# Attention ahead of two matrix stages: keys loaded a chunk earlier, x and operand casts placed later, one chunk's output stage in units of three blocks

## The chip, the cores and the metric

The kernel runs on one core of a Trainium2 chip. The metric is the device time of one execution in microseconds (us). The core has five engines with an instruction queue each: PE (matrix multiply), DVE (vector), ACT (scalar, activation tables), POOL (GpSimd) and SP, which here issues every DMA transfer. An engine works its queue off in order; an instruction that waits holds everything behind it on the same engine. Engines wait for each other, and for DMA landings, by semaphores.

## The reference

All arrays are float32; there are 8 batches, 8 heads, 576 positions and 64 values per head.

```python
k_p = k.reshape(B, H, S // 8, 8, D).mean(axis=3)
v_p = v.reshape(B, H, S // 8, 8, D).mean(axis=3)
scores = (1 / np.sqrt(D)) * np.matmul(q, k_p.transpose(0, 1, 3, 2))
attn = np.exp(scores - np.max(scores, axis=-1, keepdims=True))
attn = attn / (np.sum(attn, axis=-1, keepdims=True) + 1e-09)
x = np.matmul(attn, v_p)      # heads joined: x is 4608 x 512
gate = 1.0 / (1.0 + np.exp(-(x @ w_gate)))       # 512 x 1536
x = gate * (x @ w_val) @ w_out                   # 1536 x 512
h = x @ w_in                                     # 512 x 2048
out = (h * np.cos(h)) @ w_out2                   # 2048 x 512
```

## The kernel before

The 4608 tokens are worked in nine chunks of 512, called c = 0 to 8; a chunk boundary does not fall on a batch boundary, so a chunk's attention uses the keys of two batches. A float32 product is made of three PE passes: each operand is split into a high part (a cast, "high") and the rest (a subtraction, "low", always by the helper on line 65), and high x high, high x low and low x high are added in PSUM. Except where the inputs are still plain, the large products use a scheme with 7 block products in place of 8, so sums and differences of operand blocks are formed on DVE and POOL, written to DRAM and fetched back.

The stages follow each other on PE.

- **Attention with gate and value** (to 521 us). For chunk c the function `half_steps(c)` walks 12 half-steps; each is 12 matmuls of 128x512 (one block of the gate, `pg`, or of the value product, `pv`). After each half-step's matmuls stand the pieces that `plan(c+1)` puts there for the attention of the next chunk: loads of q, k and v (`q_load`, `kv_load`), pooling of eight rows (`kv_pool`, on POOL), transposing the pooled keys (`k_step`: PE `pk` and `pkr`, then DVE `kbd`), scores (`psc`), softmax, the transposed weights (`a_step`: `pa`, `par` to `aT`), the product with the values (`x_step`: `px`, split to `xT`, in two pieces) and the casts of the pooled values (`v_step`: `vm`, `vRp`, `vr`). A piece has a half-step number and, inside it, a priority; `put_early` places one in the window before. SP, POOL, ACT and DVE get their instructions in that same written order. The block results g are stored to `od`; of every second one POOL forms four differences `tg` (four instructions on line 755, in a tile with one buffer), whose store is put two half-steps on. The third key load (`raw_k_2`) and the third value load (`raw_v_2`) share the tile tag `kvrest`, which has one buffer.
- **Gate groups** (521 to 806 us): `g_block`, seven products per block of four chunk pairs; its operands xg are fetched, cast on ACT (`x_high`, line 1002) and split on DVE (`x_low`) at places that a table gives as (block, position).
- **w_out units** (806 to 1089 us): `half_step` takes blocks of g (`up`) fetched back from `od` and casts and splits them two blocks at a time. Groups come in the order 1, 0, 2, 3, 4, where group 0 is one chunk alone (256 columns in place of 512). Beside them run steps on the next weights (`i2_begin` and what follows it). Results `ok` are stored to `xd`; `HOMES` names the memory each lies in.
- **h stage** (1089 to 1452 us): `h_block`, the product with w_in of the second layer, then the sine on ACT; operands x by the same two functions at a table's places; sums `s_S` on POOL.
- **y stage** (1452 to 1818 us): `y_chunk`; its weights `wy` are loaded from `yd` by `load_last`, cast by `last_high` on ACT and split by `last_low` on POOL.

## Time and profile before

| | us |
|---|---|
| median of three runs | 1818.41 (1817.71 to 1825.63) |
| the profiled execution | 1819.77 |
| its span from first to last instruction | 1818.0 |

The engines were busy: PE 94 % of the span, DVE 65 %, ACT 52 %, POOL 37 %. PE's granted clock has two levels, 1.2 and 2.4 GHz; the profile gives it as a share of the full one, so 0.50 is 1.2 GHz throughout, and 0.93 over a stretch is a mean. A stretch's idle time of PE is its length less PE's busy time. In a row of the timeline the bracket at the end gives how long the engine stood idle ahead of the row, and what ended that.

### The profile page before, as it was taken

Reading aid. Unit: us, or ns where it says so; the run is one execution under the profiler, and the core shown is the slowest. Engines: PE = TensorE matmul, PEld = TensorE weight load, DVE = VectorE, ACT = ScalarE, POOL = GpSimd, SP = SyncE. Lnnn points to the kernel's source line nnn. Section 1 sums busy time; section 2 is a strip of 40 time slices with the busy share of each in tenths; the row PEclk is TensorE's granted clock in tenths of the full one; section 3 lists DMA queues with packets and bytes.
Section 4 is the critical chain, followed back from the end, with each engine's and each line's share of the span. In section 5 each row is a group of like instructions: output and inputs, shape, how many; then the busy total and the mean of one; then the engine's idle time right before and its main releaser. Section 6 shows DMA issues by size and latency. Waiting matters only on the chain. (4 is left out here: it accounts for less than half of the span.)

```text
span 1818.0 us, 27457 instructions
## 1 busy us (share of the span) xinstructions
PE 1704.9 (94%) x9432; PEld 1427.3 (79%) x9432; DVE 1184.9 (65%) x1775; ACT 951.4 (52%) x1850; POOL 674.5 (37%) x731
## 2 busy tenths in 40 slices
PE   7898998999999898999899998999999989999999
PEld 6776776777788776887778887888887878888887
DVE  7757565655585544566866686677777766565665
ACT  6454444444453443455554476677767854434433
POOL 3556566652363444340000003566757870000000
PEclk8899998999999999999999999999999989999999
DMA  9465567775469676668888876586778887666663
GB/s 255 128 209 167 172 206 246 209 224 169 155 234 307 219 241 227 214 209 285 267 266 275 263 244 211 171 268 207 259 232 290 283 284 251 225 206 218 209 216 124
DMA packets 305195, 411.04 MB, mean 226 GB/s; under 512 B 57504, under 2 KB 235424, under 8 KB 305056
## 3 DMA queue, kind: packets, MB, share of 16 engines
q1 hardware_dynamic: 305056, 409.29, 70.0%
q8 instruction: 75, 1.23, 0.3%
q14 instruction: 64, 0.52, 0.1%
HBM read 235.93 MB, written 173.28 MB: 225 GB/s over the span
## 5 line engine op out<-in xcount | busy, mean ns | idle before, releaser
L1090 POOL TENSOR_TENSOR s_S<-z_a,z_a 128x512 f32<-128x512 f32 (+1 forms) x78 | 99.3, 1294 | 393.5 <-DVE z_a L1074 393.5
L65 DVE TENSOR_TENSOR sp<-sp,sp 128x1024 fp32r<-128x1024 f32 x126 | 152.3, 1249 | 97.2 <-ACT sp L1293 97.2
L65 DVE TENSOR_TENSOR up<-up 128x1024 fp32r<-128x1024 f32 (+1 forms) x105 | 117.7, 1125 | 76.5 <-ACT up L895 75.8
L895 ACT CAST up<-up 128x1024 fp32r<-128x1024 f32 (+1 forms) x105 | 100.7, 964 | 101.2 <-DMA up<-od 80.7
L1380 PE MATMUL py_A<-wy,sp 128*128 128x512 f32 x432 | 135.7, 395 | 0.0
L1039 PE MATMUL pha<-x,hw 128*128 128x512 f32 (+1 forms) x320 | 120.5, 376 | 4.6 <-DVE z_a L1074 2.1
L1293 ACT CAST sp<-sp 128x1024 fp32r<-128x1024 f32 x126 | 123.9, 1056 | 0.0
L1043 PE MATMUL pha<-x,hw 128*128 128x512 f32 (+1 forms) x320 | 118.3, 370 | 0.0
L1044 PE MATMUL pha<-x,hw 128*128 128x512 f32 (+1 forms) x320 | 118.2, 369 | 0.0
L1070 ACT ACTIVATE z_a<-z_a 128x512 f32<-128x512 f32 (+1 forms) x160 | 94.4, 590 | 34.0 <-DVE z_a L1063 32.2
L755 POOL TENSOR_TENSOR tg<-g 128x256 f32<-128x256 f32 x54 | 53.3, 986 | 154.4 <-DMA od<-tg 84.3
L1172 PE MATMUL pga<-xg,gw 128*128 128x512 f32 (+1 forms) x240 | 90.9, 379 | 17.8 <-ACT pg L1206 15.3
L539 ACT ACTIVATE e<-psc,mx 128x72 f32<-128x72 f32 x256 | 57.9, 337 | 90.9 <-DVE mx L535 90.9
L755 POOL TENSOR_TENSOR tg<-g,g 128x256 f32<-128x256 f32 x54 | 52.5, 971 | 139.9 <-DVE g L731 139.6
L1090 POOL TENSOR_TENSOR s_S<-z_a,s_S 128x512 f32<-128x512 f32 (+1 forms) x78 | 96.2, 1233 | 3.4 <-DMA sd<-s_S 0.4
L708 PE MATMUL pg<-xT,wg 128*128 128x512 f32 (+1 forms) x228 | 93.3, 409 | 3.9 <-ACT e L560 2.7
L755 POOL TENSOR_TENSOR tg<-g,tg 128x256 f32<-128x256 f32 x108 | 94.7, 877 | 4.2
L1385 PEld LDWEIGHTS py_A<-wy,sp 128*128 128x128 f32 x432 | 81.1, 188 | 19.2
L708 PE MATMUL pv<-xT,wv 128*128 128x512 f32 (+1 forms) x228 | 94.2, 413 | 0.4 <-DVE g L731 0.4
L918 PE MATMUL po_A<-up,so 128*128 128x512 f32 (+1 forms) x240 | 90.2, 376 | 3.6 <-DVE up L65 3.4
L710 PE MATMUL pg<-xT,wg 128*128 128x512 f32 (+1 forms) x228 | 89.9, 394 | 3.4 <-DVE wg L65 3.4
L917 PE MATMUL po_A<-up,so 128*128 128x512 f32 (+1 forms) x240 | 89.1, 371 | 2.6 <-ACT up L895 2.6
(223 smaller groups left out, 5146.8 us busy)
## 6 DMA issues: line engine op xcount, KB each, us to landing
sp<-sd SPq DMA_DIRECT2D x126, 512.0 KB
up<-od SPq DMA_DIRECT2D x168, 256.0 KB
sd<-s_S SPq DMA_DIRECT2D x128, 256.0 KB
od<-tg SPq DMA_DIRECT2D x54, 512.0 KB
sd<-z_a SPq DMA_DIRECT2D x96, 256.0 KB
raw_o<-in_moe_w_out_dram SPq DMA_DIRECT2D x28, 512.0 KB
xg<-gd SPq DMA_DIRECT2D x28, 512.0 KB
x<-xd SPq DMA_DIRECT2D x28, 512.0 KB
```

Source lines behind the costliest of these rows:

```text
L65: engine.tensor_tensor(out=lo, in0=x, in1=hi.bitcast(F32), op=ALU.subtract)
L708: nc.tensor.matmul(p, wh, x[:, 0, kb], start=kb == 0, stop=False)
L755: nc.gpsimd.tensor_tensor(out=t[:, k], in0=x, in1=y, op=ALU.subtract)
L895: nc.scalar.copy(hi, lo.bitcast(F32))
L1039: nc.tensor.matmul(p, wh, x[:, 0, kb], start=k in (0, 3) and kb == 0, stop=False, skip_group_check=True,)
L1043: nc.tensor.matmul(p, wh, x[:, 1, kb], start=False, stop=False, skip_group_check=True)
L1044: nc.tensor.matmul(p, wl, x[:, 0, kb], start=False, stop=kb == 1, skip_group_check=True)
L1070: nc.scalar.activation(z, z, AF.Sin, scale=TURN)
L1090: engine.tensor_tensor(out=z[name], in0=z[x], in1=z[y], op=op)
L1172: nc.tensor.matmul(p, wh, x[:, 0, kb], start=k in (0, 3) and kb == 0, stop=False, skip_group_check=True,)
L1293: nc.scalar.copy(hi[:, r], lo[:, r].bitcast(F32))
L1380: nc.tensor.matmul(p, x[0][:, m, s], w, start=fresh and m == 0, stop=False, skip_group_check=True,)
```

## The change

- **Attention.** The key loads of chunk c+1 go from the end of the window before and its own start to half-steps 6 and 7 of the window before; pooling of keys goes to half-steps 9 and 10 there, `k_step` from half-step 3 or 4 to half-step 0. Value loads go from half-step 3 to 0 and 1, their pooling from 4 to 3. The first piece of `x_step` comes one half-step later than before after its last tile, `v_step` at half-step 8 or 9 in place of 7 or later and always on DVE. The raw copy of x (`x_keep`) is made inside `x_step`.
- **Gate and h stage operands.** The places of fetch, cast and split change; in the h stage most splits of x go from DVE to POOL, and POOL's four sums are put in two parts.
- **w_out.** Group 0 goes in 14 units of three blocks, each fetched by one transfer, cast and split in one instruction; the other groups stay at two blocks. The steps for the next weights start their two transfers two units apart and their further steps one unit later. The order of `HOMES` changes, and one small sine is put on ACT ten units after the last of these steps begins.
- **y start.** All weights are loaded in the last h group; the last fourteen are split on DVE.

```diff
-    x_late, x_raw = [], {}
-
-    def x_keep():
-
-        while x_late:
-            c, i, c0, n, p = x_late.pop(0)
             if c not in x_raw:
                 x_raw[c] = [
                     wp.tile([P, 2, C], F32, tag=f"w{NSLOT - 6 + h}", name=f"xr{c}_{h}")
                     for h in range(2)
                 ]
             nc.scalar.copy(x_raw[c][i // 2][:, i % 2, c0:c0 + n], p)
+
+    x_raw = {}
...
@@ -779,7 +775,7 @@
         steps = [[] for _ in range(NF)]
         early = [[] for _ in range(NF)]
         tiles = [(c, n) for n in range(TILES)]
-        at_ = {1: (3, 4, 6, 7), 2: (0, 2, 4, 5), 3: (0, 2, 4, 5)}.get(c, (0, 1, 3, 5))
+        at_ = {1: (3, 4, 6, 7), B - 1: (0, 1, 2, 4)}.get(c, (0, 1, 3, 5))
 
         def put(f, fn, *args):
             steps[f].append(lambda: fn(*args))
...
@@ -796,32 +792,30 @@
         if c < B:
             for g in range(3):
                 if c > 1:
-                    (put_early if g < 2 else put)(NF - 2 if g < 2 else 0, kv_load, k, c, "k", g)
-                if c > 1:
-                    put(3, kv_load, v, c, "v", g)
-                put(2 if c == 1 else int(g == 2), kv_pool, c, "k", g, nc.gpsimd)
-                put(4, kv_pool, c, "v", g, nc.gpsimd)
+                    put_early(6 + (g > 0), kv_load, k, c, "k", g)
+                    put_early(9 + (g == 2), kv_pool, c, "k", g, nc.gpsimd)
+                    put(0 if g < 2 else 1, kv_load, v, c, "v", g)
+                    put(3, kv_pool, c, "v", g, nc.gpsimd)
+                else:
+                    put(2, kv_pool, c, "k", g, nc.gpsimd)
+                    put(4, kv_pool, c, "v", g, nc.gpsimd)
         order_ = []
         for n, t in enumerate(tiles):
             f = at_[n]
-            order_.append((f, 2, q_step, (t,)))
+            order_.append((f, 1 if c == 1 else 2, q_step, (t,)))
             order_.append((f + 1, 2, s_step, (t,)))
             order_.append((f + 4, 1.5, a_step, (t,)))
 
         if c < B:
-            order_.append((3 if c < 4 else 4, 0, k_step, (c,)))
-        if nt:
-            f = at_[nt - 1] + 4
-            for i in range(KB):
-                order_.append((f, 3, x_step, (c, 0, i)))
-            order_.append((f, 3, x_keep, ()))
+            order_.append((4 if c == 1 else 0, 0, k_step, (c,)))
+        f = at_[nt - 1] + 5
+        for i in range(KB):
+            order_.append((f, 3, x_step, (c, 0, i)))
         if c < B:
-            f = max(7, at_[nt - 1] + 5) if nt else 7
-            order_.append((f, 4, v_step, (c, nc.vector if f > 8 else nc.gpsimd)))
+            order_.append((max(8, f), 4, v_step, (c, nc.vector)))
             f = NF - 2 if 1 < c < B - 1 else NF - 1
             for i in range(KB):
                 order_.append((f, 5, x_step, (c, 1, i)))
-            order_.append((NF - 1, 6, x_keep, ()))
         order_.append((NF - 1, 7, lambda: afterwards(2, lambda: x_save(c)), ()))
         for f, _, fn, args in sorted(order_, key=lambda s: (s[0], s[1])):
             put(f, fn, *args)
...
@@ -836,12 +830,11 @@
         (3, 2, "A", False), (5, 5, "B", True), (6, 3, "A", False),
     )
     OG = [1, 0, 2, 3, 4]
-    units = [(g, n, m) for g in OG for n in range(len(O_PRODUCTS)) for m in range(STEPS)]
+    units = [
+        (g, n, tuple(range(m, m + w))) for g in OG for n in range(len(O_PRODUCTS))
+        for w in [3 if g == 0 else 2] for m in range(0, HF, w)
+    ]
...
+    def unit_fetch(k, part=None):
+
+        if k >= len(units):
+            return
+        g, n, ms = units[k]
+        t, some = up_of(k), range(len(ms))
+        if g and part is not None:
+            some = [part] if part < len(ms) else []
+        elif part:
+            some = []
+        if g == 0 and some:
             nc.sync.dma_start(
-                up_of(v)[:, 1, :width(g)].bitcast(F32).rearrange(
-                    "p (i n) -> p i n", i=len(GROUPS[g])
-                ),
-                od[g][O_PRODUCTS[n][1], :, m],
+                t[:, :, 1].bitcast(F32), od[g][O_PRODUCTS[n][1], :, ms[0]:ms[-1] + 1, 0]
             )
-            count["fetched"] += 1
+            return
+        for i in some:
+            nc.sync.dma_start(
+                t[:, i, 1].bitcast(F32).rearrange("p (i n) -> p i n", i=2),
+                od[g][O_PRODUCTS[n][1], :, ms[i]],
+            )
...
@@ -917,13 +923,21 @@
             nc.tensor.matmul(p, wh, x[:, 0], start=first, stop=False, skip_group_check=True)
             nc.tensor.matmul(p, wh, x[:, 1], start=False, stop=False, skip_group_check=True)
             nc.tensor.matmul(p, wl, x[:, 0], start=False, stop=final, skip_group_check=True)
-        (unit_low if v % 2 else unit_high)(v // 2 + 2)
-        half_fetch(v + 2 * len(up))
+        if i == 0:
+            unit_high(k + 2)
+        elif i == 1:
+            unit_low(k + 2)
+        far = k + len(up)
+        if far < len(units):
+            if len(ms) == len(units[far][2]) == 2:
+                unit_fetch(far, i)
+            elif i == len(ms) - 1:
+                unit_fetch(far)
         if final:
...
     o_keep = {}
-    HOMES, free = {}, list("fbcade")
+    HOMES, free = {}, list("aebcdf")
     for g in OG:
         HOMES.update({(g, n): tag for n, tag in zip((0, 1, 2, "S2", 6), free)})
         free = [free[5], free[1], free[2], free[0], free[3], free[4]]
...
@@ -1078,18 +1092,19 @@
         def store(self, name):
             h_store(self.g, self.m, name, self.z[name])
 
-        def sums(self, engine):
+        def sums(self, engine, part):
             z = self.z
+            some = slice(2 * part, 2 * part + 2)
             for name, x, y, op in (
                 ("S3", "a11", "a21", ALU.subtract), ("S1", "a21", "a22", ALU.add),
                 ("S2", "a22", "S3", ALU.subtract), ("S4", "a12", "S2", ALU.subtract),
-            ):
+            )[some]:
                 z[name] = hp_.tile(
                     [P, C], F32, tag="s", name=f"s{self.g}_{self.m}_{name}", bufs=6
                 )[:, :self.n]
                 engine.tensor_tensor(out=z[name], in0=z[x], in1=z[y], op=op)
-            for n, name in enumerate(("S3", "S1", "S2", "S4")):
-                at_(2 + n + n // 2, lambda name=name: self.store(name))
+            for n, name in enumerate(("S3", "S1", "S2", "S4")[some]):
+                at_(2 + n + 2 * part, lambda name=name: self.store(name))
...
@@ -1388,9 +1405,8 @@
                     )
             after(n)
             y_fetch(7 * c + n + (4 if c == 0 else 5))
-            last_high(3)
-            last_low()
-            load_last(3)
+            last_high(4 if n < 2 else 3)
+            last_low(nc.vector)
             y_split(7 * c + n + 2)
...
@@ -1632,7 +1648,7 @@
             if j < 2:
                 at = (0, 0, (None, 0, 1)) if j == 0 else (0, 2, (None, 0, 1))
             else:
-                at = ((1, 0), (1, 3), (2, 0), (2, 3), (5, 2))[j - 2] + ((0, 6, 8),)
+                at = ((1, 0), (1, 3), (2, 0), (2, 3), (5, 2))[j - 2] + ((0, 8, 9),)
             m, pos, (d0, d1, d2) = at
             if d0 is not None:
                 put(0, m, pos + d0, lambda j=j: g_next(1, j))
...
@@ -1641,9 +1657,9 @@
         for g in range(1, final):
             for j in range(7):
                 if j < 3:
-                    m, at = NB - 4 + j, (0, 4, 5)
+                    m, at = NB - 4 + j, (-3, 4, 5)
                 else:
-                    m, at = NB - 1, ((0, 4, 6), (1, 5, 7), (3, 7, 8), (4, 9, 10))[j - 3]
+                    m, at = NB - 1, ((0, 6, 7), (1, 8, 9), (3, 9, 10), (4, 12, 13))[j - 3]
                 put(g, m, at[0], lambda g=g, j=j: g_next(g + 1, j))
                 put(g, m, at[1], lambda g=g, j=j: x_high(("g", g + 1), ORDER[j]))
                 put(g, m, at[2], lambda g=g, j=j: x_low(("g", g + 1), ORDER[j], nc.vector))
...
@@ -1751,8 +1768,9 @@
         for m in range(PAIRS):
             b = 3 + 5 * m + (6 if m >= PAIRS - 2 else 0)
             for n, fn in (
-                (0, lambda m: i2_begin(m, *raw_home[m])), (4, i2_exponent), (5, i2_bits),
-                (6, i2_scale), (7, i2_sums),
+                (0, lambda m: i2_begin(m, 0, *raw_home[m])),
+                (2, lambda m: i2_begin(m, 1, *raw_home[m])), (5, i2_exponent), (6, i2_bits),
+                (7, i2_scale), (8, i2_sums),
             ):
                 at_(b + n, lambda fn=fn, m=m: fn(m))
...
@@ -1812,13 +1835,13 @@
         for g in range(final):
             for j in range(7):
                 if g == 0:
-                    m, at = (j, (0, 5, 8)) if j < 6 else (PAIRS - 1, (1, 9, 10))
+                    m, at = (j, (0, 5 if j else 7, 8)) if j < 6 else (PAIRS - 1, (1, 9, 10))
                 elif j < 3:
-                    m, at = PAIRS - 4 + j, (0, 4, 4)
+                    m, at = PAIRS - 4 + j, (-3, 4, 8)
                 else:
-                    m, at = PAIRS - 1, ((0, 4, 4), (1, 5, 6), (3, 7, 8), (4, 9, 9))[j - 3]
+                    m, at = PAIRS - 1, ((0, 4, 4), (1, 5, 5), (3, 7, 8), (4, 9, 9))[j - 3]
                 high = nc.gpsimd if g and j == 6 else None
-                low = nc.gpsimd if g and j in (4, 6) else nc.vector
+                low = nc.vector if j in ((3, 5) if g else (6,)) else nc.gpsimd
                 put(g, m, at[0], lambda g=g, j=j: next_fetch(g + 1, j))
                 put(g, m, at[1], lambda g=g, j=j, e=high: x_high(g + 1, ORDER[j], e))
                 put(g, m, at[2], lambda g=g, j=j, e=low: x_low(g + 1, ORDER[j], e))
...
@@ -1827,10 +1850,10 @@
 
             def weights(m=m, n=n):
                 y_slots.extend(h_tags[n - (4 if m % 2 else 3):n])
-                load_last(2)
-                for n in (7, 10):
+                load_last((2, 2, 3, 4, 4, 4, 4, 5)[m])
+                for n in (7, 10) if m < PAIRS - 1 else ():
                     at_(n, lambda: last_high(1))
-                    at_(n + 1, last_low)
+                    at_(n + 1, lambda: last_low(nc.gpsimd))
 
             put(final, m, 9, weights)
         put(final, 1, 5, lambda: y_fetch(0))
```

The lines left out pass `unit_fetch` and `unit_step` where `half_fetch` and `half_step` stood, and add the small sine on one element.

Where it shows in the instruction order. On SP, in the window in which chunk 3's blocks are made and chunk 4's attention, before (od2 is the store of g blocks, tg3_0 the first set of differences of chunk 3, xs1 the sums of x, raw_k5 the keys of the fifth batch after the first):

```order
125 L758 DMA od2_79<-tg3_0_2652 128x4x256
126 L664 DMA xs1_a11_2938<-gd1_84 128x1024
127 L664 DMA xs1_a21_2940<-gd1_84 128x1024
128 L664 DMA xs1_a22_2942<-gd1_84 128x1024
129 L761 DMA od2_79<-g3_7_2820 128x2x256
130 L498 DMA q5_0_2971<-in_q_dram 128x8x64
131 L498 DMA q5_1_3018<-in_q_dram 128x8x64
132 L412 DMA raw_k5_0_3020<-in_k_dram 64x2x512 x2
133 L412 DMA raw_k5_1_3023<-in_k_dram 64x2x512 x2
134 L746 DMA od2_79<-g3_2_2923 128x256
135 L758 DMA od2_79<-tg3_1_2918 128x4x256
136 L498 DMA q5_2_3078<-in_q_dram 64x8x64 x2
```

and now:

```order
125 L742 DMA od2_79<-g3_1_2678 128x256
126 L414 DMA raw_k5_1_2907<-in_k_dram 64x2x512 x2
127 L419 DMA raw_k5_2_2910<-in_k_dram 64x1x512
128 L754 DMA od2_79<-tg3_0_2673 128x4x256
129 L660 DMA xs1_a11_2946<-gd1_84 128x1024
130 L660 DMA xs1_a21_2948<-gd1_84 128x1024
131 L660 DMA xs1_a22_2950<-gd1_84 128x1024
132 L757 DMA od2_79<-g3_7_2785 128x2x256
133 L500 DMA q5_0_2979<-in_q_dram 128x8x64
134 L500 DMA q5_1_3038<-in_q_dram 128x8x64
135 L742 DMA od2_79<-g3_2_2918 128x256
136 L754 DMA od2_79<-tg3_1_2913 128x4x256
```

The last key load, which shares its buffer with the value rest that `v_step` casts one half-step later, has moved ahead of the store of tg3_0.

On POOL in the same window, before (vRp and vr belong to `v_step`, so22 are sums for another weight matrix):

```order
150 L65 TENSOR_TENSOR vm_103<-vS4_2672,vm_103 64x4x64 x2
151 L65 TENSOR_TENSOR vRp4_2908<-raw_v4_2_2636,vRp4_2908 32x64 x4
152 L470 TENSOR_TENSOR vr_104<-vRp4_2908,mask_100 128x512
153 L755 TENSOR_TENSOR tg3_1_2918<-g3_1_2657 128x256
154 L755 TENSOR_TENSOR tg3_1_2918<-g3_7_2820,g3_1_2657 128x256
155 L755 TENSOR_TENSOR tg3_1_2918<-g3_7_2820,tg3_1_2918 128x256 x2
156 L200 TENSOR_TENSOR so22_3051<-ro22_3026 128x256
```

and now:

```order
143 L751 TENSOR_TENSOR tg3_1_2913<-g3_7_2785,tg3_1_2913 128x256 x2
144 L401 TENSOR_TENSOR raw_k5_0_2872<-raw_k5_0_2872 128x2x256
145 L401 TENSOR_TENSOR raw_k5_0_2872<-raw_k5_0_2872 128x2x128
146 L401 TENSOR_TENSOR kS5_2981<-raw_k5_0_2872 128x128
147 L401 TENSOR_TENSOR raw_k5_1_2907<-raw_k5_1_2907 128x2x256
148 L401 TENSOR_TENSOR raw_k5_1_2907<-raw_k5_1_2907 128x2x128
149 L401 TENSOR_TENSOR kS5_2981<-raw_k5_1_2907 128x128
150 L401 TENSOR_TENSOR raw_k5_2_2910<-raw_k5_2_2910 64x256
151 L401 TENSOR_TENSOR raw_k5_2_2910<-raw_k5_2_2910 64x128
152 L401 TENSOR_TENSOR kR5_2982<-raw_k5_2_2910 64x64
```

The pooling of the keys (kS, kR) now stands directly behind the differences tg3_1, ahead of tg3_2; `v_step` has left POOL.

On DVE beside group 0 of the w_out stage, before (up is an operand unit, raw_i the next weights, ok a result):

```order
880 L322 TENSOR_TENSOR raw_i24_8392<-raw_i24_8392 128x256 x4
881 L65 TENSOR_TENSOR up1_7546<-up1_7546 128x2x256
882 L65 TENSOR_TENSOR up2_7547<-up2_7547 128x2x256
883 L982 TENSOR_TENSOR ok0_2_8525<-po0_B0_8402,ok0_2_8525 128x256
884 L982 TENSOR_TENSOR ok0_2_8525<-po0_B1_8403,ok0_2_8525 128x256
885 L65 TENSOR_TENSOR up3_7861<-up3_7861 128x2x256
```

and now:

```order
886 L65 TENSOR_TENSOR up3_7861<-up3_7861 128x3x256
887 L65 TENSOR_TENSOR hw4_8463<-raw_i21_8066,hw4_8463 128x2x256
888 L65 TENSOR_TENSOR up0_7545<-up0_7545 128x3x256
889 L324 TENSOR_TENSOR raw_i23_8266<-raw_i23_8266 128x256 x4
890 L65 TENSOR_TENSOR up1_7546<-up1_7546 128x3x256
891 L65 TENSOR_TENSOR hw5_8515<-raw_i21_8066,hw5_8515 128x2x256
```

The split of a unit now covers three blocks, and the work on the next weights stands between the units at a coarser step.

## Rows read from the trace of the kernel before

**Rows 1.** The page: busy time and share of each engine.

```profile
PE 1704.9 (94%) x9432; PEld 1427.3 (79%) x9432; DVE 1184.9 (65%) x1775; ACT 951.4 (52%) x1850; POOL 674.5 (37%) x731
```

**Rows 2.** Stretches by stage: length, busy of five engines, clock, DMA share, GB/s.

```profile
102.00:482.00 380.00, 343.33 (x2399) 278.58 (x2398) 231.44 (x441) 172.96 (x516) 206.69 (x271) 0.93 0.62 190
...
521.00:806.00 285.00, 265.93 (x1252) 221.65 (x1250) 160.19 (x206) 122.41 (x209) 127.55 (x133) 0.98 0.74 247
806.00:1089.00 283.00, 267.86 (x1269) 222.19 (x1268) 202.41 (x276) 157.72 (x215) 9.27 (x7) 0.99 0.80 261
1089.00:1452.00 363.00, 352.90 (x1681) 294.72 (x1680) 269.06 (x425) 261.41 (x481) 232.87 (x205) 0.99 0.73 239
1452.00:1818.00 366.00, 354.36 (x2019) 308.25 (x2017) 221.73 (x260) 162.10 (x215) 35.00 (x35) 0.98 0.67 218
```

**Rows 3.** Waits of PE, 52 to 521 us: total us, times, longest us.

```profile
PE px L618 <- DVE aT L65: 15.8, 10, 2.7
PE psc L523 <- DVE kbd L451: 13.0, 8, 4.7
```

**Rows 4.** Timeline of SP: start, length, instruction; stores of the differences.

```profile
231.63 0.44 SPq L758 DMA_DIRECT2D od<-tg  x1
...
253.22 0.42 SPq L758 DMA_DIRECT2D od<-tg  x1
```

**Rows 5.** Timeline of POOL: key pooling, and the next differences after those stores.

```profile
222.76 2.11 POOL L399 TENSOR_TENSOR raw_k<-raw_k 128x512 f32<-128x512 f32 x2
...
229.94 0.31 POOL L399 TENSOR_TENSOR kR<-raw_k 64x64 f32<-64x64 f32 x1
...
236.74 0.73 POOL L755 TENSOR_TENSOR tg<-g 128x256 f32<-128x256 f32 x1 [6.48 <-DVE aT L65]
...
259.62 0.74 POOL L755 TENSOR_TENSOR tg<-g 128x256 f32<-128x256 f32 x1 [0.95 <-DMA od<-tg]
```

**Rows 6.** Timeline of ACT: the casts of `v_step`.

```profile
253.99 0.83 ACT L461 CAST vm<-vS 64x256 fp32r<-64x256 f32 x2
...
255.19 0.50 ACT L467 CAST vRp<-raw_v 32x64 fp32r<-32x64 f32 x2
```

**Rows 7.** Timeline of PE: first matmuls of half-steps 8 and 9, end of the next half-step 0.

```profile
253.18 0.47 PE L708 MATMUL pg<-xT,wg 128*128 128x512 f32 x1
...
256.01 0.39 PE L708 MATMUL pv<-xT,wv 128*128 128x512 f32 x1
...
269.53 0.60 PE L508 MATMUL pq<-ident,q 128*128 128x128 f32 x4
```

**Rows 8.** Timeline of PE, gate stage: the first matmul behind a pause.

```profile
623.23 0.79 PE L1172 MATMUL pga<-xg,gw 128*128 128x512 f32 x1 [5.25 <-ACT pg L1206]
```

**Rows 9.** Timeline of ACT ahead of that pause.

```profile
619.55 1.04 ACT L1002 CAST xg<-xg 128x1024 fp32r<-128x1024 f32 x1 [8.16 <-DMA xg<-gd]
```

**Rows 10.** Stretches of w_out: group 0, and the head of group 2.

```profile
869.10:911.60 42.50, 33.63 (x254) 31.02 (x252) 34.88 (x70) 25.01 (x46) 0.00 (x0) 1.00 0.81 274
911.60:928.00 16.40, 13.31 (x49) 9.74 (x48) 9.72 (x16) 8.58 (x13) 0.00 (x0) 0.90 0.92 319
```

**Rows 11.** Timeline of PE at the start of the h stage.

```profile
1097.51 0.58 PE L1039 MATMUL phb<-x,hw 128*128 128x256 f32 x1 [4.99 <-ACT z_a L1055]
```

**Rows 12.** Timeline of ACT there.

```profile
1097.08 0.37 ACT L1055 COPY z_a<-phb 128x256 f32<-128x256 f32 x1 [6.31 <-DMA xd<-ok]
...
1098.04 1.28 ACT L1070 ACT_TABLE_LOAD   x1
```

**Rows 13.** Timeline of POOL: sums in an h block, weights at the y start.

```profile
1112.95 1.44 POOL L1090 TENSOR_TENSOR s_S<-z_a,z_a 128x256 f32<-128x256 f32 x2 [3.12 <-DVE z_a L1074]
...
1474.22 2.77 POOL L65 TENSOR_TENSOR wy<-wy 128x256 fp32r<-128x256 f32 x4 [4.32 <-DMA wy<-yd]
1476.96 3.38 POOL L65 TENSOR_TENSOR wyb<-wyb 128x256 fp32r<-128x256 f32 x2
```

**Rows 14.** Timeline of PE at the y start.

```profile
1476.49 1.19 PE L1380 MATMUL py_B<-wy,sp 128*128 128x512 f32 x2 [7.26 <-POOL wy L65]
```

More of the change, by code (lines that the diff above doesn't have):

```diff
@@ L73, in attention_two_mlps @@
     edge = ctx.enter_context(tc.tile_pool(name="edge", bufs=1, side="right"))
-    nc.gpsimd.memset(edge.tile([P, 24], F32, name="edge"), 0.0)
+    edge_words = edge.tile([P, 24], F32, name="edge")
+    nc.gpsimd.memset(edge_words, 0.0)
     gt = tc.alloc_tile_pool(name="gt", bufs=1, side="right")
@@ L287, in attention_two_mlps, with i2_begin @@
     i2_raw, hw = {}, {}
-    def i2_begin(m, pool, tag):
-        t = pool.tile([P, 2, 512], I64, tag=tag, name=f"raw_i2{m}")
-        for i, j in enumerate((m, m + PAIRS)):
-            nc.sync.dma_start(
-                t[:, i].rearrange("p (kb c) -> p kb c", kb=KB),
-                w2_in[:, j * P:(j + 1) * P].rearrange("(kb p) c -> p kb c", p=P),
-            )
-        i2_raw[m] = [t[:, i] for i in range(2)]
+    def i2_begin(m, i, pool, tag):
+        if i == 0:
+            t = pool.tile([P, 2, 512], I64, tag=tag, name=f"raw_i2{m}")
+            i2_raw[m] = [t[:, i] for i in range(2)]
+        j = m + i * PAIRS
+        nc.sync.dma_start(
+            i2_raw[m][i].rearrange("p (kb c) -> p kb c", kb=KB),
+            w2_in[:, j * P:(j + 1) * P].rearrange("(kb p) c -> p kb c", p=P),
+        )
     def i2_exponent(m):
@@ L838, in attention_two_mlps @@
     OG = [1, 0, 2, 3, 4]
-    units = [(g, n, m) for g in OG for n in range(len(O_PRODUCTS)) for m in range(STEPS)]
+    units = [
+        (g, n, tuple(range(m, m + w))) for g in OG for n in range(len(O_PRODUCTS))
+        for w in [3 if g == 0 else 2] for m in range(0, HF, w)
+    ]
     PER = len(O_PRODUCTS) * STEPS
-    halves_of = [
-        (g, n, m) for g in OG for n in range(len(O_PRODUCTS)) for m in range(HF)
-    ]
-    count = {"fetched": 0}
     o_weights, o_tags, up = [], [], []
@@ L870, in width, with up_of @@
         return HALF * len(GROUPS[g])
-    def up_of(v):
-        return up[v // 2 % len(up)][:, v % 2]
-    def half_fetch(upto):
-        while count["fetched"] < min(upto + 1, len(halves_of)):
-            v = count["fetched"]
-            g, n, m = halves_of[v]
+    def up_of(k):
+        t, (g, _, ms) = up[k % len(up)], units[k]
+        if g == 0:
+            t = t.rearrange("p i h n -> p (i h n)").rearrange("p (i h n) -> p i h n", i=4, h=2)
+        return t[:, :len(ms)]
+    def unit_fetch(k, part=None):
[8 more added lines that the diff above has]
+        if g == 0 and some:
             nc.sync.dma_start(
-                up_of(v)[:, 1, :width(g)].bitcast(F32).rearrange(
-                    "p (i n) -> p i n", i=len(GROUPS[g])
-                ),
-                od[g][O_PRODUCTS[n][1], :, m],
-            )
-            count["fetched"] += 1
+                t[:, :, 1].bitcast(F32), od[g][O_PRODUCTS[n][1], :, ms[0]:ms[-1] + 1, 0]
+            )
+            return
+        for i in some:
+            nc.sync.dma_start(
+                t[:, i, 1].bitcast(F32).rearrange("p (i n) -> p i n", i=2),
+                od[g][O_PRODUCTS[n][1], :, ms[i]],
+            )
     def unit_of(k):
-        t = up[k % len(up)]
-        return (t[:, :, i, :width(units[k][0])] for i in range(2))
+        t = up_of(k)
+        return (t[:, :, i] for i in range(2))
     def unit_high(k):
@@ L911, in half_step @@
         w = o_weights[STEPS * n + m // 2][:, m % 2]
-        x = up_of(v)[..., :width(g)]
+        x = up_of(k)[:, i]
         first, final = fresh and m == 0, m == HF - 1
@@ L1132, in h_block @@
         if a:
-            a.sums(nc.gpsimd if b else nc.vector)
+            a.sums(nc.gpsimd if b else nc.vector, 0)
         if b:
@@ L1136, in h_block @@
         after(5)
+        if a:
+            a.sums(nc.gpsimd if b else nc.vector, 1)
         if b:
@@ L1733, in attention_two_mlps @@
         now[0] = 0
-        half_step(2)
-        half_step(3)
+        unit_step(1, 0)
+        unit_step(1, 1)
         gx[0].release()
@@ L1775, in x_first_low, with sine_table @@
             split_lo(nc.vector, t[:, :, 1], t[:, :, 1].bitcast(F32), t[:, :, 0])
+        def sine_table():
+            one = edge_words[:, :1]
+            nc.scalar.activation(one, one, AF.Sin)
+        at_(LAST + 10, sine_table)
         first_x = {}
@@ L1781, in attention_two_mlps @@
         now[0] = 2
-        for v in range(4, len(halves_of)):
-            half_step(v)
-            if v % 2:
-                due()
+        for k in range(2, len(units)):
+            for i in range(len(units[k][2])):
+                unit_step(k, i)
+            due()
         op_.release()
```

21 lines of the change are left out of this document (11 added, 10 removed).

## The prediction

> **What bounds the kernel now.** I read the page first: PE is busy for 94 % of the span [rows 1], so an edit can win only what PE loses by standing still or by running at the lower clock. Next come the stretches by stage, to see where that is [rows 2]. PE's idle time, length less busy, is 36.7 us in the attention windows from 102 to 482 us, 19.1 in the gate groups, 15.1 in w_out, 10.1 in the h stage and 11.6 in the y stage. The clock column shows where PE ran slow. In the attention windows the mean is 0.93, and 0.07 of 380 us is 27 us that full clock would have saved had PE been busy throughout; it was busy for 343 of them and some of the slow stretches are the idle ones, so I count 18. In the gate groups the same product is 5.7 us. Last come the waits and, at each pause, the timeline, for what PE waited for. In attention these are the transposed weights aT ahead of `px`, 15.8 us, and `kbd` ahead of the scores, 13.0 us [rows 3]. In the other stages single pauses carry most: 5.25 us in a gate group, twice [rows 8]; 4.99 us at the h start [rows 11]; 7.26 us at the y start [rows 14]; in w_out a group 0 of 42.5 us in which PE was busy for 33.6 [rows 10].
>
> **Attention: what goes.** `k_step` stands at half-step 0 and the scores come behind another 12 matmuls, so `kbd` has a half-step (253.18 to 256.01, 2.8 us [rows 7]) of cover that it hadn't: the 13.0 us go. The first piece of `x_step` comes one half-step later, which covers aT: each wait was at most 2.7 us [rows 3], as long as one half-step, so most of the 15.8 us go too. With small waits of the same sort I count 33 of the 36.7 us idle as removed and 3.7 as staying, and all 18 us of lost clock with them, 51 us together.
>
> **Attention: what comes.** The load of the last keys, raw_k_2, is written behind half-step 7. Its buffer is that of raw_v_2, which `v_step` reads behind half-step 8. So SP stands at this load until `v_step`'s casts are done, and behind it on SP is the store of the first differences. POOL's next differences need that store landed, since tg has one buffer; behind them on POOL stands the pooling of all three key loads; and behind that, on PE, `k_step`. The price, on the clock of the window around 253 us: half-step 8 begins at 253.18 [rows 7], its matmuls end at 256.01, and the tanh takes ACT to about 256.7 (a cast of twice its columns takes 1.04 [rows 9]). `v_step`'s casts run from 253.99 to 255.69 in the trace, 1.7 us [rows 6], so here to 258.4, and DVE's splits of the same data, estimated as long as the last 0.87 us of these casts, to 259.3. SP's load and the issue of the store bring 259.9. From the issue of a store to POOL's next differences the trace has 5.1 us (231.63 to 236.74) and 6.4 (253.22 to 259.62) [rows 4, 5], so 265.0 to 266.3. The differences are four of 0.73, 2.9 us, and the pooling of keys 7.5 us (222.76 to 230.25) [rows 5]: 275.4 to 276.7. PE's work from half-step 8 to the end of the next half-step 0 ends at 269.53 [rows 7], and has the same pieces after the change. So `k_step` stalls PE for 5.9 to 7.2 us; I take 6.5. It comes in six windows (k loads for the second to the seventh further batch): 39 us. PE's clock falls after such pauses: in the gate groups, whose pauses are as long as these, 5.7 us of clock stand beside 19.1 idle, 0.3 to one, so 12 us more. New cost 51, removed 51: I take nothing for this stage. The bounds: if POOL's chain is not late, 45 us are won (6 left of small waits); if the store lands as slowly as would make each stall 12 us, 6 x 12 x 1.3 = 94 comes and 43 are lost.
>
> **Gate groups.** The cast of xg stood 8.16 us on ACT until its transfer landed [rows 9], and behind it on ACT the copy that PE waited for [rows 8]. It now stands three products later. Products take 6 matmuls, half of a half-step, 1.4 us, so ACT would arrive 4.2 us later; the transfer does not come earlier, since SP is held at the same place by another load, and the work that ACT does in those 4.2 us is what was late. Left of 5.25 us is between 1.0 and all of it; I take 2.8, because the tanh and cast work behind has still to be caught up. That is 2.5 us at each of two pauses, and of the 5.7 us of clock I count 2.5: 7.5 us won (bounds 2 and 13).
>
> **w_out.** Group 0 took 42.5 us with PE busy for 33.6, DVE for 34.9 and the DMA engines at 0.81 [rows 10]. Three blocks per instruction make 14 splits of 768 columns in place of 21 of 512, the same columns with a third fewer starts, and fewer steps for the next weights stand beside it. DVE's work beside it stays near 34.9, and with a little slack for waits I take 36.5: 6 us won, bounded by 0 and by PE's idle 8.9. The head of group 2 has 3.1 us idle and 0.10 of 16.4 us clock [rows 10], 4.7 together, from the same lateness; I take 2.5. The start of the stage has its up transfers placed better, 1 us. Together 9.5 us (0 to 16). An edit costed at nothing here: i2 steps one unit later, hidden as PE waits for up only; without that cover the h stage's first weights are late by a unit, 2.7 us.
>
> **h start and h stage.** The copy on ACT waited 6.31 us for an earlier result's store, because the memory was shared [rows 12], and PE 4.99 us for it [rows 11]. With another order of `HOMES` that wait goes. What is late next is the first sine: its table load, 1.28 us on ACT [rows 12], is made in advance. I keep 1 us of the pause, count 4.0 + 1.3, and 0.7 for clock: 6 us (3 to 8). In the h stage each x split moves to POOL as four instructions of 0.72 us, about 2.9, beside the sums of 2.9 [rows 13]. A block of half width gives POOL twice 1.44 us of sums and 3.12 idle, 6.0 together, so 5.8 us just fit: I take nothing, with 5 us lost as the bound.
> The Trainium skill ("SBUF — State Buffer", section "SBUF: two separate sides") says that an instruction of GpSimd and one of VectorE with two SBUF inputs lock each other out for their whole length. A POOL split takes 1.69 us beside DVE's splits at the y start, against 0.72 for a sum of the same shape in an h block [rows 13], which agrees for the first place and shows no lock at the second. By the rule, moved splits would cost the h stage something; that is the third rival.
> The Trainium skill ("ScalarE: Activation LUTs", section "What ACT_TABLE_LOAD costs") puts a switch of tables at about 1.28 us and as much again for a drain, 2.66 us. The trace has the 1.28, and ACT goes on right behind it; by the page the term would be 1.4 us more.
>
> **y start.** POOL's splits of wy waited 4.32 us for their transfer, then ran 2.77 us, and PE waited 7.26 [rows 13, 14]. The transfers now come in the h stage, so the 4.32 go. On DVE, four weights' splits stand ahead of those of the operand sp: eight of about 0.37 us, an estimate by half of 0.73 for the same shape, 3 us. I count 3.3 us of the pause and 0.7 us of clock: 4 us (0 to 7).
>
> **The sum.** 0 - 7.5 - 9.5 - 6 - 4 = -27. Against the profiled execution's 1819.8 us (span 1818.0, 1.8 outside) that is 1792.8. The median of the runs lies 1.4 us below it, so I predict 1791 us.
>
> **Rivals.** *The key chain is not late* (chance 0.25): if `v_step` runs sooner than I think, or the differences' store lands in the 5 us or less that leave POOL free, `k_step` finds its keys ready. For it: the stall is the difference of long times, and half-step 8 to `k_step` is 16.4 us. Against it: each link has its row, and 5.9 us is already the sum with the short ones. 27 + 45 = 72 off: 1746.
> *The key chain is later still* (0.13), the way to slower: SP's hold also delays the xs and q transfers behind it, and each store waits longer at the windows of highest DMA load. It decides from where it eats the other stages' 27 us: new cost 78 in place of 51, a stall of 10 us with 3 of clock in each window. For it: at 231 to 260 us stores already take 6.4. At 12 us the stage loses 43: 1791 + 43 = 1834.
> *The h stage becomes POOL's* (0.07): if half of POOL's four moved splits take the 1.69 us seen beside DVE in place of 0.72 [rows 13], POOL's 5.8 of 6.0 us become 7.7, and the six blocks with moved splits in the first group lose about 2 us each: 1791 + 12 = 1803. Against it: the sums' 0.72 us.
> *The edits behind attention don't do what they say* (0.07): pauses go on with the next-late transfer and give half: 1804 to 1808.
> My forecast has the rest, 0.48, with its own range 1776 to 1808.
>
> **How the numbers follow.** Half a per cent, 9 us, is about what a measurement here can tell from no change, so faster is below 1809. The forecast (0.48) and the first rival (0.25) are there, bar 0.04 at the edge, and so are most of the third and fourth, 0.10: 0.79, of which I shift 0.03 upward for a stall of 9 to 10 us: 0.76. The second rival is split: 0.12 slower, and 0.12 are left for within. The range reaches from 1744, the first rival with 2 us below, to 1821, which leaves out the late half of the second rival.
>
> **What would show it.** Right: in the windows of chunks 1 to 6, PE `pk` or `pkr` waits for POOL's kS or kR by 5 to 8 us, POOL tg waits for od<-tg just before, and SP idles ahead of the raw_k_2 load; `px` and `psc` waits nearly gone; group 0 within 35 to 38 us; `phb` at the h start without a wait for xd<-ok; `py_B` pausing for about 4 us. Wrong: `pk` without waits, or an h block beyond 6.1 us.

## The result and the profile after

The changed kernel takes 1801.92 us (median of four runs, 1800.33 to 1804.64) against 1818.06 before: a ratio of 0.9903, 95 % interval 0.9874 to 0.9933. The forecast was 1791, in a range of 1744 to 1821. The sign and the range held; the sum did not come about as forecast.

Stages, in us, from PE's first matmul of each to the first of the next, in the profiled executions (span 1818.0 and 1798.6):

| stretch | before | after | difference | forecast |
|---|---|---|---|---|
| up to chunk 1's blocks | 102.4 | 105.9 | +3.5 | |
| seven attention windows | 385.7 | 399.7 | +14.0 | 0 |
| chunk 8's blocks | 32.6 | 32.6 | 0 | |
| gate groups | 285.8 | 275.6 | -10.1 | -7.5 |
| w_out (group 0 within it) | 282.7 (42.5) | 274.6 (36.1) | -8.1 (-6.3) | -9.5 (-6) |
| h stage | 363.2 | 349.5 | -13.7 | -6 |
| y stage | 365.6 | 360.6 | -5.0 | -4 |

So the stages behind attention win 37 us, 10 more than forecast, and 17.5 are given back up to their start. Of these, 14.0 lie in the seven windows; the 3.5 ahead of them are not shown to be the change's, since four kernels among the experiments that have the same code up to there took 102.5 to 105.3. Stretches of the changed kernel (columns as in [rows 2]; the last line is group 0, which answers to [rows 10]):

```profile
102.00:500.00 398.00, 344.87 (x2414) 273.95 (x2415) 236.69 (x477) 174.16 (x517) 181.73 (x240) 0.94 0.61 186
538.00:814.00 276.00, 264.90 (x1257) 221.22 (x1256) 163.72 (x210) 124.65 (x212) 132.92 (x136) 0.99 0.76 255
...
1088.50:1438.00 349.50, 346.98 (x1682) 292.67 (x1681) 252.81 (x410) 262.98 (x480) 266.19 (x265) 1.00 0.78 253
1438.00:1798.60 360.60, 353.09 (x2017) 307.53 (x2015) 225.21 (x288) 161.32 (x215) 7.33 (x7) 0.99 0.66 216
878.00:914.10 36.10, 32.24 (x253) 30.61 (x252) 31.49 (x56) 22.72 (x39) 0.00 (x0) 1.00 0.96 330
```

PE idles for 53 us in the attention stretch (398.0 less 344.9), where [rows 2] had 36.7 in 380, and for 2.5 in the h stage, where it had 10.1. PE's waits in the attention stage of the changed kernel, beside [rows 3]:

```profile
PE pk L446 <- POOL kS L401: 19.0, 9, 4.0
PE px L620 <- DVE aT L65: 11.8, 10, 2.6
PE pkr L447 <- POOL kR L401: 9.1, 5, 4.0
PE pq L510 <- ACT e L541: 4.3, 3, 2.1
```

The 13.0 us for `kbd` are gone, 28 us for the keys have come, and `px` still waits for aT. One window's chain in the changed kernel, on SP, DVE, POOL and PE (columns as in [rows 4, 5, 7]; the first row of PE begins half-step 8):

```profile
254.16 1.36 SPq L414 DMA_DIRECT2D raw_k<-in_k_dram  x2
267.53 0.63 SPq L419 DMA_DIRECT2D raw_k<-in_k_dram  x1
268.20 0.45 SPq L754 DMA_DIRECT2D od<-tg  x1
...
266.56 0.91 DVE L65 TENSOR_TENSOR vRp<-raw_v,vRp 32x64 fp32r<-32x64 f32 x4
...
272.44 0.74 POOL L751 TENSOR_TENSOR tg<-g 128x256 f32<-128x256 f32 x1 [20.76 <-DMA od<-tg]
...
275.35 2.17 POOL L401 TENSOR_TENSOR raw_k<-raw_k 128x512 f32<-128x512 f32 x2
...
284.46 0.31 POOL L401 TENSOR_TENSOR kR<-raw_k 64x64 f32<-64x64 f32 x1
...
261.61 0.47 PE L704 MATMUL pg<-xT,wg 128*128 128x512 f32 x1
...
282.36 0.51 PE L446 MATMUL pk<-ident,kS 128*64 128x128 f32 x2 [3.52 <-POOL kS L401]
284.83 0.31 PE L447 MATMUL pkr<-ident,kR 64*64 64x64 f32 x1 [1.95 <-POOL kR L401]
```

SP stands from 255.5 to 267.5 at the last key load, until DVE's last read of raw_v for `v_step` ends (266.56 + 0.91). POOL idles for 20.8 us until the store behind it has landed (4.2 us after its issue), then sums and pools, and PE waits for each part as it comes.

### The profile page after: what moved, and what is told of

Read it like the earlier page. It is cut to its first block, busy times and chain, and to the rows that moved or that the text cites. A ratio compares the mean times of both kernels' runs of the same rounds, so it can differ in the third digit from the quotient of the medians.

```text
span 1798.6 us, 27384 instructions
## 1 busy us (share of the span) xinstructions
PE 1694.7 (94%) x9432; PEld 1417.1 (79%) x9432; DVE 1176.1 (65%) x1823; ACT 954.9 (53%) x1844; POOL 651.4 (36%) x721
## 4 chain that ended last, share of the span: by engine, by line
PE 55%; DMA 4%; DVE 2%; issue 1%; ACT 1%; POOL 1%; SPq 0%; DVEq 0%; ACTq 0%; POOLq 0%
PE py_A L1397 7%; PE py_B L1397 4%; PE py_A L1402 3%; PE pha L1053 3%; PE pha L1057 3%; PE pha L1058 3%; PE po_A L924 2%; PE po_A L925 2%; PE po_A L923 2%; PE py_B L1402 2%; DMA up<-od 2%; PE po_B L924 2%; PE po_B L925 2%; PE po_B L923 2%; PE py_C L1397 2%; PE phb L1058 2%
## 5 line engine op out<-in xcount | busy, mean ns | idle before, releaser
L65 POOL TENSOR_TENSOR x<-x 128x256 fp32r<-128x256 f32 x84 | 60.1, 748 | 271.3 <-ACT x L1016 271.0
L1105 POOL TENSOR_TENSOR s_S<-z_a,z_a 128x512 f32<-128x512 f32 (+1 forms) x78 | 94.3, 1230 | 67.3 <-DVE z_a L1088 67.3
L924 PE MATMUL po_A<-up,so 128*128 128x512 f32 (+1 forms) x240 | 89.6, 373 | 4.4 <-DVE up L65 4.2
```

Source lines behind the costliest of these rows:

```text
L65: engine.tensor_tensor(out=lo, in0=x, in1=hi.bitcast(F32), op=ALU.subtract)
L924: nc.tensor.matmul(p, wh, x[:, 1], start=False, stop=False, skip_group_check=True)
L1105: engine.tensor_tensor(out=z[name], in0=z[x], in1=z[y], op=op)
```

## The experiments

Every ratio is to the kernel before, run on the same chip. The kernel before took 1818.1 to 1821.2 us (medians) beside the groups of experiments, so times of different groups that lie 3 us apart are not told apart. Lists of PE's waits begin at 52 us for the changed kernel and for two buffers alone, at 100 us for the other attention experiments.

**The shared buffer.**

```diff
-            raw = at.tile([P, 1, 512], F32, tag="kvrest", name=name)
+            raw = at.tile([P, 1, 512], F32, tag="kvrest", name=name, bufs=2)
```

> The changed kernel with two buffers for the tile that the last key load and the last value load share, and nothing else. Theory K (SP is held at the last key load until v_step has read that buffer, and so the store of the differences, POOL's key pooling and k_step come late): PE's waits at pk and pkr for POOL fall from 28 us to under 6, SP no longer stands 10 us ahead of that load, the attention windows become 30 to 38 us shorter, the whole about 1768 us. Rival P (POOL reaches the key pooling late in any case, because its differences wait for g and for their own store): pk and pkr keep 3 us or more in each window, and the whole stays at 1790 or above.

1785.33 us, 0.9818 (0.9788 to 0.9848). The waits for keys are gone altogether. The seven windows take 382.3 us in place of 399.7 (in the profiled execution, which took 1791.8), but that is still only 3 less than before the change. PE's largest waits up to the gate stage, and one of them with DVE and POOL ahead of it:

```profile
PE px L620 <- DVE aT L65: 26.9, 11, 5.4
PE pq L510 <- ACT e L541: 4.3, 3, 2.1
```

```profile
205.48 2.25 DVE L65 TENSOR_TENSOR vm<-vS,vm 64x256 fp32r<-64x256 f32 x2 [1.07 <-ACT vm L463]
207.74 2.98 DVE L65 TENSOR_TENSOR vRp<-raw_v,vRp 32x64 fp32r<-32x64 f32 x4
210.83 0.69 DVE L472 TENSOR_TENSOR vr<-vRp,mask 128x512 fp32r<-128x512 f32 x1
...
214.69 0.68 DVE L65 TENSOR_TENSOR aT<-pa,aT 128x512 fp32r<-128x512 f32 x1
...
205.28 2.17 POOL L401 TENSOR_TENSOR raw_k<-raw_k 128x512 f32<-128x512 f32 x2
...
215.43 0.74 PE L620 MATMUL px<-aT,vm 128*128 128x320 f32 x2 [5.10 <-DVE aT L65]
```

Theory K holds for the wait; its total was 17 us too low, since `px`'s waits for aT grew from 11.8 to 26.9. `v_step`'s splits stand on DVE in front of aT's, and while POOL pools keys the two of vm take 1.1 us each here, where the changed kernel needs 0.42.

**Old attention, new rest; and new attention, old rest.** The first is the changed kernel with the hunks on `x_step`, `x_keep` and `plan` undone, the second the kernel before with those three alone.

> The changed kernel with the attention plan, x_step and x_keep of the kernel before; gate, w_out, h and y parts as changed. If the attention part alone costs what the stages show (its stretch ends 17.5 us later than before), the whole comes to about 1784 us with an attention stretch ending near 521 us, and the later stages keep their 37 us of gain. Rival: the later stages owe part of their gain to the new attention order (what is loaded or left over at its end); then less than 30 us of gain stays and the whole is above 1788.

1779.85 us, 0.9774 (0.9747 to 0.9802).

> The kernel before with the attention part of the change alone. If the parts add up, about 1836 us, with pk and pkr waiting some 28 us for POOL. If the attention part is neutral by itself and the loss comes from something else, 1815 to 1822.

1842.28 us, 1.0126 (1.0102 to 1.015). The two agree: the attention part costs 22.1 us one way (1801.92 - 1779.85) and 22.5 the other. About 13.5 of it lies in the seven windows (386.2 and 399.1 us), the rest spread over the stretch ahead of them and the stages behind: the gate groups take 272.6 us behind the old attention, 275.6 behind the new.

**The x piece later still**, on top of two buffers.

```diff
-        f = at_[nt - 1] + 5
+        f = at_[nt - 1] + 6
```

> The changed kernel with two buffers for the shared tile, and the first piece of x_step (and v_step with it where that comes later) one half-step later still. In the changed kernel px still waits 14 us for aT, cast and split by ACT and DVE. Theory A (those waits are aT a half-step late): px waits fall below 5 us and the whole is 8 to 12 us under the kernel with two buffers alone. Rival (once SP isn't held, DVE and ACT are no longer late and px hardly waits in either): within 4 us of it. Rival on the other side: v_step and the later x piece crowd the window's end, and it is slower by 3 to 8 us.

1782.04 us, 0.9794 (0.9765 to 0.9822), not told apart from two buffers alone. Between the theories: `px` waits 11.2 us for aT in place of 23.1 (both from 100 us on), but 5.0 and 6.6 have come for vr and vm.

```profile
PE px L620 <- DVE aT L65: 11.2, 6, 3.7
PE px L620 <- ACT vm L463: 6.6, 3, 2.4
PE px L620 <- DVE vr L472: 5.0, 3, 1.8
```

**`v_step` back on POOL**, on top of two buffers.

```diff
-            order_.append((max(8, f), 4, v_step, (c, nc.vector)))
+            order_.append((max(8, f), 4, v_step, (c, nc.gpsimd)))
```

> The changed kernel with two buffers for the shared tile, and v_step's splits back on POOL, at the new half-step 8 or 9. With two buffers alone px waits 23 us for aT, and ahead of the worst of these waits (5.1 us at 215 us) DVE spends 6.0 us on v_step's splits, which stand before aT's. Theory L (v_step on DVE, made longer by POOL's key pooling beside it, holds aT): px waits for aT fall to 12 us or less, the whole about 1773 us, 10 to 14 under the 1785 of two buffers alone; POOL's key pooling comes 4 us later, within the 7 to 9 us that kR is now early. Rival M (aT is late by the softmax ahead of it): px waits stay over 18 us and the whole within 4 us of 1785. Rival on the other side: POOL is full, pk waits again for some 4 us a window, and the whole is 1790 or above.

1776.50 us, 0.9748 (0.9729 to 0.9768). Theory L: of `px`'s 23.1 us of waits for aT 2.8 are left, and smaller ones for POOL come.

```profile
PE px L620 <- POOL vr L472: 6.6, 4, 2.7
...
PE px L620 <- DVE aT L65: 2.8, 7, 1.1
PE pkr L447 <- POOL kR L401: 2.8, 2, 1.6
```

The attention mended in this way beats the old one with the same rest (1779.85 us) by 3 us, which the intervals do not separate: its seven windows are 9.6 us shorter (376.6 against 386.2), and the gate groups and w_out behind them 5 longer.

**POOL's key pooling a half-step later**, on top of two buffers, `v_step` on DVE.

```diff
-                    put_early(9 + (g == 2), kv_pool, c, "k", g, nc.gpsimd)
+                    put_early(10 + (g == 2), kv_pool, c, "k", g, nc.gpsimd)
```

> The changed kernel with two buffers for the shared tile, and the key pooling one half-step later (10 and 11 in place of 9 and 10), so that it runs less beside v_step on DVE. If DVE's instructions of two SBUF operands and POOL's shut each other out (theory L's second half), DVE's vm splits go from a median of 0.80 us towards their shortest, 0.42, px waits fall by some 5 us, and the whole is about 1780. If the lengthening has another cause, vm stays near 0.8 and the whole near 1785. Key pooling 2.7 us later uses up part of the 7 us by which keys are early; pk does not wait.

1778.45 us, 0.9763 (0.9742 to 0.9784). The splits of vm on DVE, count and shortest, median and longest in ns, in the changed kernel, with two buffers, and with the pooling later:

```profile
L65 DVE TENSOR_TENSOR vm<-vS,vm x14: 409/420/424, 93.0 to 452.9; 64x256 fp32r<-64x256 f32 x14
```

```profile
L65 DVE TENSOR_TENSOR vm<-vS,vm x14: 417/800/1420, 95.6 to 437.8; 64x256 fp32r<-64x256 f32 x14
```

```profile
L65 DVE TENSOR_TENSOR vm<-vS,vm x14: 416/507/1420, 93.6 to 431.2; 64x256 fp32r<-64x256 f32 x14
```

In the changed kernel POOL stands idle while `v_step` runs in all six windows from chunk 1's on, in five of them for want of the store behind SP's hold. No split is lengthened there: `v_step` keeps DVE busy for 2.4 us each time, 14.4 in all. With two buffers POOL works beside it in these five, mostly on keys, and `v_step` takes 29.0 us in all; in the sixth it stays at 2.4. Against these 14.6 us more, `px`'s waits for aT in the windows grow by 13.5 (9.3 to 22.8). So the hold that cost 28 us of key waits also kept DVE free, and taking it away won 17 and not 30.

Moving POOL's work away brings the median down. It frees `v_step` in one window only, that of chunk 2:

```profile
204.97 0.85 DVE L65 TENSOR_TENSOR vm<-vS,vm 64x256 fp32r<-64x256 f32 x2 [1.07 <-ACT vm L463]
```

There `v_step` falls from 5.9 to 2.4 us, and `px`'s waits in all by 3.3 (23.1 to 19.8), which shows the link for one window; for the others it rests on the sums above. By the Trainium skill ("SBUF — State Buffer", section "SBUF: two separate sides") a DVE instruction with two SBUF inputs and a POOL instruction that reads SBUF shut each other out for a whole instruction. The trace agrees: the split takes 0.42 us without POOL beside it and up to 1.42 with. The seven windows are 5.7 us shorter (376.6 against 382.3), with 34 us at 1.2 GHz in place of 41. That part of it is not shown to come from the edit: the two runs with `v_step` on POOL at half-step 8, the one above and the last of the y stage below, have the same attention code, and yet 38 and 27 us at 1.2 GHz and windows of 376.6 and 372.7.

**The h stage's two parts.** First the changed kernel with the old operand table, splits on DVE and sums in one piece; then with the old memory homes alone:

```diff
-    HOMES, free = {}, list("aebcdf")
+    HOMES, free = {}, list("fbcade")
```

> The changed kernel with the h stage's table of operand places, its splits on DVE and its four sums in one piece as before. The h stage went from 363.2 to 349.5 us where 6 us were forecast. If the new places and POOL's splits give the part not forecast: the h stage about 356 us, the whole about 1808. If the new memory homes and the early table load give all of it: h within 1.5 us of 349.5, the whole at 1802.

1807.13 us, 0.9923 (0.9899 to 0.9948), h stage 356.2 us.

> The changed kernel with the old order of HOMES alone. If the shared memory was what held the first copy of the h stage: the 5 us pause of phb for ACT's copy behind xd<-ok comes back, with 1 to 3 us of lower clock, h about 356 us, the whole about 1808. Rival (another order of stores late in w_out, given by the new units, has already freed that memory in time): no pause, 1802.

1807.20 us, 0.992 (0.99 to 0.994), h stage 357.2. PE's largest wait in the h stage of each, the places' first:

```profile
PE pha L1053 <- DVE z_a L1088: 3.5, 6, 1.6
```

```profile
PE phb L1053 <- ACT z_a L1069: 6.9, 1, 6.9
```

With the old homes ACT waits again for the store of an earlier result:

```profile
1094.73 0.37 ACT L1069 COPY z_a<-phb 128x256 f32<-128x256 f32 x1 [8.19 <-DMA xd<-ok]
```

So the places give 6.7 us and the homes 7.7, together 14.4. That is the stage's 13.7 within its scatter: 348.9 to 352.4 us in the experiments that leave it as changed. Both whole times lie 5 us above the changed kernel's with intervals that overlap, so it is the stage's length that shows the two parts. A block of the kernel before, with DVE's split of x in it, and POOL in the first blocks of the changed kernel:

```profile
1116.15 1.22 DVE L65 TENSOR_TENSOR x<-x 128x1024 fp32r<-128x1024 f32 x1
...
1119.02 1.44 POOL L1090 TENSOR_TENSOR s_S<-z_a,z_a 128x256 f32<-128x256 f32 x2 [3.12 <-DVE z_a L1074]
```

```profile
1099.25 1.43 POOL L1105 TENSOR_TENSOR s_S<-z_a,z_a 128x256 f32<-128x256 f32 x2
1100.64 1.54 POOL L1105 TENSOR_TENSOR s_S<-z_a,s_S 128x256 f32<-128x256 f32 x2
1102.15 2.83 POOL L65 TENSOR_TENSOR x<-x 128x256 fp32r<-128x256 f32 x4
1104.94 1.44 POOL L1105 TENSOR_TENSOR s_S<-z_a,z_a 128x256 f32<-128x256 f32 x2
```

POOL works without a gap and keeps up with a block that has shortened to 5.7 us (1104.94 - 1099.25) from 6.07 (1119.02 less the 1112.95 of [rows 13]): with the split of 1.22 us gone from DVE, PE's waits for DVE's z_a fall from the 3.5 us of the old places to 0.6. By POOL's sums five such blocks make 1.7 of the 6.7 us; 1.9 lie ahead of the first, 1.8 in the shorter last one and the rest behind, where the causes were not separated.

**Group 0 in units of two.**

```diff
-        for w in [3 if g == 0 else 2] for m in range(0, HF, w)
+        for w in [2] for m in range(0, HF, w)
```

> The changed kernel with group 0 of the w_out stage in units of two blocks, as before; the steps for the next weights as changed. Theory W (fewer, larger instructions and transfers make the gain in group 0): 36.1 us go back to 41 or more, the whole about 1807. Theory I (fewer steps for the next weights beside group 0, and their later start, make it): group 0 stays within 2 us of 36, the whole near 1802. My forecast held DVE's work to be the bound in both.

1862.74 us, 1.0232 (1.0207 to 1.0256). This tells nothing of either theory, and its time is no measure of units of two: the rule that issues the fetch behind the last block of a unit holds only where two units differ in size, and here the fetch is issued behind the first block. So in group 0, and in the units of group 1 that fetch for it, second blocks are computed from the operands of a later unit, and PE waits for each landing:

```profile
PE po_A L924 <- DMA up<-od: 25.8, 9, 6.0
PE po_B L924 <- DMA up<-od: 19.3, 8, 2.6
```

What in group 0 made its 6.3 us, larger units or fewer steps beside it, stays open.

**`v_step` on POOL at half-step 7**, on top of the kernel with it at 8.

```diff
-            order_.append((max(8, f), 4, v_step, (c, nc.gpsimd)))
+            order_.append((max(7, f), 4, v_step, (c, nc.gpsimd)))
```

> The changed kernel with two buffers, v_step's splits on POOL, and v_step allowed at half-step 7 (which moves it for three of the windows, those of the second to fourth batch). px waited 6.6 us for POOL's vr and pk and pkr 4.4 us for POOL's keys with v_step at 8: if both are POOL's lateness, half of them go, and the whole is 1770 to 1774. If other waits take their place, within 3 us of 1776.

1775.91 us, 0.975 (0.9728 to 0.9772): no difference from 1776.50. `px` waits 4.9 us for vr in place of 6.6, `pkr` 6.3 for kR in place of 2.8.

**The y stage: the engine, and the order.** First the changed kernel with the last splits on POOL; then, on top of two buffers and `v_step` on POOL, sp's split put first:

```diff
-            last_low(nc.vector)
+            last_low(nc.gpsimd)
```

> The changed kernel with the last weights' splits of the y stage back on POOL, all loads still early. The changed kernel pauses 3.6 us at its y start, for DVE's split of sp behind four pairs of weight splits. If the early loads made the gain and DVE's splits only move the wait: POOL takes 1.4 to 1.7 us for each pair beside DVE, fourteen pairs, some late by 3 us or more, sp's splits 1.66 in place of 1.18, so a pause of the same size or 2 us smaller, the whole 1799 to 1803. If DVE's speed was what it needed: pauses of 6 us or more, 1806.

1796.87 us, 0.9865 (0.9842 to 0.9889), y stage 359.6 us, a pause of 2.1.

```diff
-            last_low(nc.vector)
             y_split(7 * c + n + 2)
+            last_low(nc.vector)
```

> The changed kernel with two buffers, v_step's splits on POOL, and in the y stage sp's split ahead of the last weights' splits on DVE. The 3.6 us pause at the y start is for sp's split behind eight weight splits of 0.35 us: if order alone makes it, it falls to 1 us or less and the y stage from 360.6 to about 357, the whole about 1773. If the weights are then late in its place: y stays within 1.5 us of 360.6, the whole at 1776.

1768.35 us, 0.9711 (0.9692 to 0.973), y stage 356.4. The pause in the changed kernel, answering to [rows 14], with DVE ahead of it, and what is left of it in the last experiment:

```profile
1458.87 0.50 PE L1402 MATMUL py_B<-wy,sp 128*128 128x256 f32 x2 [3.55 <-DVE sp L65]
...
1454.92 1.42 DVE L65 TENSOR_TENSOR wy<-wy 128x256 fp32r<-128x256 f32 x4
1456.26 1.42 DVE L65 TENSOR_TENSOR wyb<-wyb 128x256 fp32r<-128x256 f32 x4
1457.61 2.35 DVE L65 TENSOR_TENSOR sp<-sp,sp 128x1024 fp32r<-128x1024 f32 x2
```

```profile
PE py_B L1402 <- DVE sp L65: 0.9, 1, 0.9
```

The early loads made the gain at the y start; the move to DVE brought none, and the order on DVE was worth 4 us more (360.6 to 356.4). The other 4 of the 8 us between this run and the one with `v_step` on POOL lie in attention windows of the same code. This last kernel is the fastest: 1768 us, 34 under the changed one.

## Why the prediction was right and wrong

- **"`k_step` stalls PE for 5.9 to 7.2 us", in six windows.** The mechanism is as told, link by link. It came in five windows (PE idles there for 7.1, 4.5, 5.8, 5.2 and 5.4 us ahead of `pk` and `pkr`), 28 us in place of 39; the first of the six has no such wait. In the window shown the hold ends 5.9 us after half-step 8 begins (261.6 to 267.5), against 6.1 in the working. The store's 4.2 us were shorter than the 5.1 to 6.4 read from [rows 4, 5], where the 5.1 was no landing: the row at 236.74 says that POOL waited for DVE. The key pooling was longer, 9.4 us (275.35 to 284.77) and not 7.5, so these two errors nearly cancel.
- **"Most of the 15.8 us go too", and 51 us removed.** This step failed. `px` still waits 11.8 us for aT, so of 33 us of idle time 17 went, 13.0 for `kbd` and 4.0 here. With the hold taken away these waits rise to 26.9 (23.1 from 100 us on), and from 100 us on 2.8 are left once `v_step` is off DVE. I had priced the move of `v_step` to DVE only as a link of the key chain, not as work that stands ahead of aT on DVE. The first rival (no late chain, 45 us won) would have failed for the same reason: with the chain gone the windows were 3 us shorter than before.
- **Lost clock, 18 us removed and 12 added.** PE's granted clock was at 1.2 GHz for 51.2 us of the seven windows before and 47.8 after, and for 54.6 to 61.4 in four experiments with the same attention code. A stretch at 1.2 GHz follows each of the five key waits. The clock followed the pauses, and PE's idle time had not become less.
- **Gate, -7.5.** Measured -10.1, and -13.2 behind the old attention: the old pauses of 5.25 us have no successor, so the 2.8 us each that I kept were too careful; a new one of 4.0 us for ACT's gz_a belongs to the new attention, and is 1.0 behind the old.
- **w_out, -9.5.** Measured -8.1, with 6.3 in group 0 against 6. DVE's work in it fell from 34.9 to 31.5 us, where I held it still; PE was busy for 32.2 of 36.1.
- **h, -6.** The homes gave 7.7, where the term has 4.7 without the table load (4.0 and 0.7 for clock); the table load was not tried alone. The places, taken as nothing, gave 6.7. I had counted POOL's load against the block's 6.0 us, but not asked what made the block 6.0, which is DVE with its splits; by the blocks that were shown this is 1.7 of the 6.7, and the rest stays open. The rival in which POOL bounds this stage did not come.
- **y, -4.** Measured -5.0, with a pause of 3.6 for sp behind weight splits, as told.
- **The side of the result.** Right in part by luck, by two errors of opposite sign: attention 14 us worse than its term in the windows (17.5 with the stretch ahead of them), the rest 10 better. That the time fell at all is owed to the edits behind attention alone.

## What to carry to other kernels

A load that waits for its buffer holds its whole queue: before moving a load ahead, look at who last reads its buffer, and at what stands behind it on the queue. A piece moved to another engine has two prices, when it ends and what it stands in front of there. When a wait is taken away, the engines that it kept idle start at once, and here that lengthened others: ask what two engines will then do side by side.

## What had not been expected of the hardware

DVE's split of 64x256 takes 0.42 us with POOL idle and up to 1.42 with POOL pooling keys. At the y start sp's splits of 128x1024 take 1.18 us with the weights' splits on DVE (2.35 for two), and 1.71 with these on POOL:

```profile
1453.68 3.42 DVE L65 TENSOR_TENSOR sp<-sp,sp 128x1024 fp32r<-128x1024 f32 x2
```
